# Attention and two expert layers on one core: the second batch's keys and values loaded ahead of the first token group, its first matmuls in halves, the transposes two steps behind the norm

## The chip, the cores and the metric

The program runs as one launch on 1 of the 8 cores of a Trainium2 chip. The metric is the device time of that core in microseconds (us), as the median of three runs. TensorE (PE in the profile, PEld for its weight loads), VectorE (DVE), ScalarE (ACT) and GpSimd (POOL) each take their own instructions in order; SyncE (SP) issues the DMAs.

## The reference, cut to what matters

```python
# attention without softmax, batch 8, 8 heads, 576 tokens, head 64
kv = einsum('bhsd,bhse->bhde', k, v)
out = einsum('bhsd,bhde->bhse', q, kv)
out = out / sqrt(mean(out * out, -1) + 1e-6) * g_norm
x = out.transpose(0, 2, 1, 3).reshape(4608, 512)
# dense layer, 512 -> 2048 -> 512
x = square(maximum(x @ w_in, 0)) @ w_out
# one of 8 experts for each token, 512 -> 1024 -> 512
logits = x @ w_gate + modality_bias[modality_id]
e = argmax(logits); gate = max of softmax(logits)
out = gate * (maximum(x @ w1[e], 0) @ w2[e])
```

All data are float32. The kernel computes a product as three matmuls: each operand is split into a high and a low part (tiles of type fp32r), and high x high, high x low and low x high are summed.

## The kernel before, in words

**Groups and steps.** The 4608 tokens are 36 tiles of 128. `BLK` sorts them into twelve groups j = 0 to 11, of 4, 3, 3, 3, 2 and then 3 tiles each. The dense layer runs group by group. A group has 16 steps i (one for each 128 of the 2048 hidden features). A step issues `emit_h(j, i)` on PE, 12 matmuls whose moving side is the whole group (512 columns in group 0, L368), and `emit_x(j, i - 2)`, 12 matmuls of 512 columns in group 0 (3 for each token tile, L416 to L418), which add feature block i - 2 to the output. Between the two stand, on ACT, `relu` (L385) and `square` (L395, L397), and on DVE `rest` (L403, in the middle groups L402 too), which makes the low part that the third matmul of `emit_x` reads. In group 0 `relu`, `square` and `rest` of feature block i - 1 are issued in step i, between pieces of weight conversion. The results of `emit_h` lie in a PSUM pool of two buffers (`ps_h`), so `emit_h` of block i + 2 waits for `relu` of block i.

**Weights.** w_in and w_out arrive in 32 pieces of 512 KB, alternating, in four buffers `wq`. Numbered n, piece 2i + 1 holds the w_in part that `emit_h(0, i + 1)` reads, piece 2i + 2 the w_out part of `emit_x(0, i)`. Each piece goes through a conversion: `w_scale` (L287 on ACT, for every fourth piece L290 and L291 too), `w_join` (L300, or L304 and L305, on DVE), `w_sum` (L314 on DVE; after it the buffer is free and SP issues the load of piece n + 4), and `w_part`, the high part on ACT (L329) and the low part on DVE (L327). In group 0 step i converts pieces 2i + 4 and 2i + 5 and begins 2i + 6 and 2i + 7.

**Attention.** Before group 0 a prologue loads k and v of batch 0 (four DMAs of 480 KB, L138, and two remainders of 192 KB, L147), multiplies them (`kv_mm`, L153), and makes the four token tiles of group 0 (`att_out` L196, `att_sq` L202, `att_sum` L206, the norm, L239 on DVE for two tiles and L592 on POOL for two, and `att_tr`: four transposes on PE, L252, then L255 on ACT and L256 on DVE, which write the high and low halves of the tile `xt`). `warm` issues matmuls without use. k and v of batch 1 are loaded during steps 0 and 1 of group 0 and multiplied in steps 1 and 2. For every group the tiles of the next are made during its steps: the n-th at step i0 the load of q, at i0 + 2 `att_one` (L196, L202, L206 and two POOL instructions), at i0 + 3 the norm (L239), at i0 + 4 the transposes, with i0 = 3n + 4 in group 0 and 3n + 3 after it. From group 1 on DVE also computes the router's logits (L440), two or three in each of steps 3 to 14.

**Other DMAs on SP's queue.** In step 2 of group 0 `tab_init` (L604) writes a table of 578 KB to DRAM, in runs of 272 bytes. All DMAs named here are issued by SP, in program order.

After the twelve groups the expert layer works through 40 slots of 128 tokens; nothing in it is touched.

Of the kernel before, what the change touches and what calls it, by code (L numbers as in the profile page):

```python
# [40 lines left out]
NKV = 2  # L41
# [4 lines left out]
def body(ctx: ExitStack, tc: tile.TileContext, qT, kvp, kvr, g_norm, w_in, w_out, mod, wg, wgd, mb, w1, w2, out):  # L46
# [80 lines left out]
    def kv_load(b, hp):  # L127

        n = 4 * (b - 1) + hp
        if b == 0 and hp == 0:  # L130
            early.append(xt_p.tile([128, 4, 2, 4, 128], F32, tag="xt0", name="early"))
        if n == 0:
            early.append(xt_p.tile([128, 3, 2, 4, 128], F32, tag="xt1", name="early"))
        if b < NKV:
            t = early[-1][0:120, n % 3 if b else hp]
        else:
            t = t4_p.tile([120, 2, 4, 128], F32, tag="t4", name="kvt")
        nc.sync.dma_start(out=t, in_=kvp[b, hp])  # L138
        kvin[b, hp] = t
        if hp % 2 == 0:  # L140
            if b == 0:
                t = early[0][0:96, hp // 2, :].rearrange("p (a b c) -> p a b c", a=2, b=2)
            elif b < NKV:
                t = g_p.tile([96, 2, 2, 128], F32, tag="ghl", name="rem")
            else:
                t = one.tile([96, 2, 2, 128], F32, tag="rem", name="rem")
            nc.sync.dma_start(out=t, in_=kvr[b, hp // 2])  # L147
            kvrem[b, hp // 2] = t
# [134 lines left out]
    def w_scale(n, c=2):  # L283

        if n < NP:
            low, up, a = w_at(n, c)
            nc.scalar.activation(out=a.bitcast(F32), in_=up.bitcast(F32), func=AF.Copy, scale=2.0**-112)  # L287
            if n % 4 == 0:
                up = up[:, 0]
                nc.scalar.activation(out=up.bitcast(F32), in_=up.bitcast(F32), func=AF.Sign, bias=tiny)  # L290
                nc.scalar.activation(  # L291
                    out=up.bitcast(I32), in_=up.bitcast(F32), func=AF.Copy, scale=2.0**30, bias=-2.0**30
                )

    def w_join(n, c=2):

        for n in range(n, min(n + c, NP)):
            low, up, a = (t[:, 0] for t in w_at(n, 1))
            if n % 4 == 0:
                nc.vector.scalar_tensor_tensor(  # L300
                    out=a, in0=a, scalar=3, in1=up, op0=ALU.logical_shift_left, op1=ALU.bitwise_or
                )
            else:
                nc.vector.tensor_scalar(out=a, in0=a, scalar1=3, scalar2=None, op0=ALU.logical_shift_left)  # L304
                nc.vector.scalar_tensor_tensor(  # L305
                    out=a, in0=up, scalar=0x80000000, in1=a, op0=ALU.bitwise_and, op1=ALU.bitwise_or
                )
# [49 lines left out]
        nc.sync.dma_start(out=wd[e, pc, :, u], in_=uhl.pop(n))  # L357


    gs = {}  # L360

    def emit_h(j, i):
        xt = xts[j]
        ps = ps_h.tile([128, 512], F32, tag="h", name="hps")
        n = 0
        for k in range(4):
            for wi, xi in ((0, 0), (0, 1), (1, 0)):
                nc.tensor.matmul(  # L368
                    ps[:, 0:128 * BLK[j]], wav[:, i, wi, k, :], xt[:, xi, k, :], start=(n == 0), stop=(n == 11)
                )  # L370
                n += 1
        hps[i] = ps
        if j > 0:
            relu(j, i)
            square(j, i)
            rest(j, i)

    hps = {}

    rs = {}  # L380

# [179 lines left out]
    for T in range(n0):  # L561
        att_out(T, *((ps_acc, "acc") if T < 3 else (ps_sm, "sm")))
        sqs.append(att_sq(T))
        if T == 0:
            w_part(0, False, 1)
        if T == 1:
            w_scale(1, 1)
    for T in range(n0):
        att_sum(sqs[T], ss[:, 8 * T:8 * T + 8])
        if T == 0:  # L570
            w_part(0, True, 1)
        if T == 1:
            w_join(1, 1)
            w_sum(1, 1)
    warm(50)
    xc = []
    for T in (2, 3):
# [1 line left out]
        nc.scalar.activation(out=x, in_=xo[T], func=AF.Copy)  # L579
        xc.append(x)  # L580
    ms = att_rms(ss, n0, True)
    w_part(1, False, 1)
    w_scale(2)
    ri = att_inv(*ms)
    for T in range(n0):
        r = ri[:, 8 * T:8 * T + 8]
# [5 lines left out]
            nc.gpsimd.tensor_tensor(out=x, in0=x, in1=r.unsqueeze(2).to_broadcast([128, 8, 64]), op=ALU.mult)  # L592
    for T in range(n0):
        att_tr(T, *((ps_acc, "acc") if T < 2 else (ps_att, "att")))
    w_part(1, True, 1)
    w_join(2)
    w_sum(2)
# [322 lines left out]
    kv_ld, kv_pr = {}, {}  # L920
    for b in range(1, 8):
        for hp in range(4):
            n = 4 * (b - 1) + hp
            if b < NKV:
                i = n // 2
                kv_ld.setdefault((0, i), []).append((b, hp))
                kv_pr.setdefault((0, i + 1), []).append((b, hp))
            else:
                j = BLOCK[b * 576 // 128] - 1
                kv_ld.setdefault((j, 2 * (hp // 2)), []).append((b, hp))  # L930
                kv_pr.setdefault((j, 2 * (hp // 2) + 2), []).append((b, hp))
# [5 lines left out]
    for j in range(NB):  # L937
        nx = [T for T in range(NTILE) if BLOCK[T] == j + 1]
        for i in range(NF):
            if j == 0:  # L940
                if i == NF - 1:
                    wg_sb = p1b.tile([128, E, 512], F32, tag="wg", name="wg_sb")
                    nc.sync.dma_start(out=wg_sb, in_=wg.unsqueeze(0).to_broadcast([128, E, 512]))
                    bias_init()
            emit_h(j, i)
            if j == 0:
                if i == 2:
                    tab_init()
# [18 lines left out]
            for a in kv_ld.get((j, i), []):  # L967
                kv_load(*a)
            for n, T in enumerate(nx):
                i0 = 3 * n + (4 if j == 0 else 3)  # L970
                if i == i0:
                    q_load(T)
                if i == i0 + 2:
                    att_one(T)
                if i == i0 + 3:
                    att_norm(T)
                if i == i0 + 4:
                    att_tr(T)
            if j > 0 and i >= 2:
                emit_x(j, i - 2)  # L980
# [159 lines left out]
```

## Time and profile before

| | |
|---|---|
| three runs | 1451.18, 1452.71, 1454.43 us, median 1452.71 |
| the profiled execution, its own time | 1453.12 us |
| its span in the trace | 1451.4 us |
| mean granted TensorE clock | 0.989 |
| PE busy | 1405.7 us, 97% of the span |
| DVE, ACT, POOL busy | 765.4, 513.8 and 430.5 us (53%, 35%, 30%) |

The span runs from the first instruction to the last; the rest of the execution's time, 1.7 us, lies outside it. "Granted clock" is the share of full speed (1.00 is 2.4 GHz, 0.50 is 1.2 GHz). Times of rows are microseconds from the start of the span. Engines wait on semaphores; a row of the timeline gives the idle time before the instruction in brackets, and what ended it.

### The profile page before, as it was taken

How to read it: one execution, taken by the hardware profiler on the slowest of the kernel's cores; microseconds unless marked ns; L12 is line 12 of the kernel's file. 1: busy time of each engine (PE TensorE's matmuls, PEld its weight loads, DVE VectorE, ACT ScalarE, POOL GpSimd, SP SyncE). 2: the span in 40 equal slices, each digit the busy share in tenths (PEclk: the TensorE clock that was granted, in tenths of full speed). 3: DMA queues.
4: the chain of work that ended last, by engine and by line, in shares of the span. 5: the costliest groups of instructions: out<-in, count | busy, mean ns of one | idle time of the engine just before them, and what ended most of it. 6: DMA issues, size and time to landing. Idle time of an engine off the chain costs nothing. (4 is left out here: it accounts for less than half of the span.)

```text
span 1451.4 us, 24693 instructions
## 1 busy us (share of the span) xinstructions
PE 1405.7 (97%) x7682; PEld 1213.2 (84%) x7682; DVE 765.4 (53%) x1578; ACT 513.8 (35%) x946; POOL 430.5 (30%) x376
## 2 busy tenths in 40 slices
PE   6789999999999999999999999999999999999997
PEld 5578888888998888888888989888888888888886
DVE  4687486858766577766758777162212222212221
ACT  4576234434424344433333443322222222222221
POOL 1003034425415244534334442222222222222210
PEclk9899999999999999999999999999999999999999
DMA  6845235566445565656565651643114623457761
GB/s 182 227 164 182 84 124 189 196 173 218 146 137 196 173 191 188 214 164 197 171 193 189 216 173 68 276 167 140 41 42 155 218 98 103 135 208 254 269 264 75
DMA packets 79440, 246.79 MB, mean 170 GB/s; under 512 B 14670, under 2 KB 14670, under 8 KB 70992
## 3 DMA queue, kind: packets, MB, share of 16 engines
q1 hardware_dynamic: 68176, 208.30, 43.8%
q0 software_dynamic: 8832, 20.09, 4.2%
q10 hardware_dynamic: 2304, 16.78, 2.9%
q8 instruction: 70, 1.15, 0.3%
q14 instruction: 58, 0.48, 0.1%
HBM read 414.33 MB, written 87.70 MB: 346 GB/s over the span
## 5 line engine op out<-in xcount | busy, mean ns | idle before, releaser
L368 PE MATMUL hps<-xt,wa 128*128 128x384 f32 (+2 forms) x2304 | 442.8, 341 | 0.8 <-ACT xt L255 0.8
L368 PEld LDWEIGHTS hps<-xt,wa 128*128 128x128 f32 x2304 | 405.5, 190 | 24.4 <-ACT xt L255 1.2
L352 POOL TENSOR_TENSOR hl<-raw,hl 128x512 fp32r<-128x512 f32 x128 | 177.9, 1396 | 261.6 <-ACT hl L351 261.2
L906 PE MATMUL yps<-wb,hq 128*128 (+1 forms) x960 | 234.2, 399 | 0.4 <-ACT hq L895 0.4
L869 PE MATMUL hps<-wa,xq 128*128 (+1 forms) x960 | 233.7, 399 | 0.0
L416 PE MATMUL acc<-wb,ghl 128*128 128x512 f32 x576 | 231.5, 402 | 0.0
L440 DVE SCALAR_TENSOR_TENSOR junk<-x,wg_sb 128x512 f32<-128x512 f32 x264 | 224.6, 851 | 4.8
L418 PE MATMUL acc<-wb,ghl 128*128 128x512 f32 x576 | 227.0, 394 | 0.0
L417 PE MATMUL acc<-wb,ghl 128*128 128x512 f32 x576 | 226.2, 393 | 0.0
L906 PEld LDWEIGHTS yps<-wb,hq 128*128 128x128 f32 x960 | 177.5, 188 | 41.1 <-ACT hq L895 0.7
L869 PEld LDWEIGHTS hps<-wa,xq 128*128 128x128 f32 x960 | 177.3, 188 | 39.6
L402 DVE TENSOR_TENSOR r<-r 128x384 f32<-128x384 f32 (+1 forms) x160 | 106.0, 663 | 184.3 <-ACT ghl L395 183.9
L385 ACT ACTIVATE r<-hps 128x384 f32<-128x384 f32 (+2 forms) x192 | 93.6, 488 | 305.1 <-PE hps L368 297.6
L403 DVE TENSOR_TENSOR ghl<-r,ghl 128x384 fp32r<-128x384 f32 (+2 forms) x192 | 139.8, 728 | 51.5 <-ACT r L397 33.5
L896 DVE TENSOR_TENSOR hq<-htp,hq 128x512 fp32r<-128x512 f32 x80 | 51.5, 686 | 206.0 <-ACT hq L895 206.0
L913 POOL DMA_INDIRECT out<-y,me x40 | 40.7, 1018 | 351.8 <-ACT y L912 287.9
L351 ACT ACTIVATE hl<-raw 128x512 fp32r<-128x512 f32 x128 | 80.1, 626 | 143.2 <-DMA raw<-w 93.6
L418 PEld LDWEIGHTS acc<-wb,ghl 128*128 128x128 f32 x576 | 108.1, 188 | 23.9
L416 PEld LDWEIGHTS acc<-wb,ghl 128*128 128x128 f32 x576 | 108.4, 188 | 18.4 <-issue 0.5
L417 PEld LDWEIGHTS acc<-wb,ghl 128*128 128x128 f32 x576 | 108.4, 188 | 17.8
L395 ACT ACTIVATE ghl<-r 128x384 fp32r<-128x384 f32 (+2 forms) x192 | 100.9, 526 | 6.1
L885 DVE TENSOR_SCALAR hr<-hps 128x512 f32<-128x512 f32 x36 | 24.9, 692 | 141.1 <-PE hps L869 141.1
(152 smaller groups left out, 1077.9 us busy)
## 6 DMA issues: line engine op xcount, KB each, us to landing
wa<-wd SPq DMA_DIRECT2D x148, 1024.0 KB
wb<-wd SPq DMA_DIRECT2D x144, 1024.0 KB
wd<-hl SPq DMA_DIRECT2D x128, 512.0 KB
raw<-w SPq DMA_DIRECT2D x128, 256.0 KB
kvt<-kvp SPq DMA_DIRECT2D x24, 480.0 KB
x2buf<-x SPq DMA_DIRECT2D x36, 256.0 KB
wq<-w_in SPq DMA_DIRECT2D x16, 512.0 KB
wq<-w_out SPq DMA_DIRECT2D x16, 512.0 KB
```

Source lines behind the costliest of these rows:

```text
L352: nc.gpsimd.tensor_tensor(out=hl[:, 1, :].bitcast(F32R), in0=t, in1=hl[:, 0, :], op=ALU.subtract)
L368: nc.tensor.matmul(ps[:, 0:128 * BLK[j]], wav[:, i, wi, k, :], xt[:, xi, k, :], start=(n == 0), stop=(n == 11))
L385: nc.scalar.activation(out=rs[i], in_=hps.pop(i)[:, 0:c], func=AF.Relu)
L395: nc.scalar.activation(out=g2[0], in_=r, func=AF.Square)
L402: nc.vector.tensor_tensor(out=r, in0=r, in1=r, op=ALU.mult)
L403: nc.vector.tensor_tensor(out=g2[1], in0=r, in1=g2[0].bitcast(F32), op=ALU.subtract)
L416: nc.tensor.matmul(a, g2[0][:, sl], wbv[:, i, 0, :], start=(i == 0), stop=False)
L417: nc.tensor.matmul(a, g2[0][:, sl], wbv[:, i, 1, :], start=False, stop=False)
L418: nc.tensor.matmul(a, g2[1][:, sl], wbv[:, i, 0, :], start=False, stop=(i == NF - 1))
L440: nc.vector.scalar_tensor_tensor(out=junk, in0=x2s[j, t], scalar=1.0, in1=wg_sb[:, e, :], op0=ALU.mult, op1=ALU.mult, accum_out=lgs[j][:, ...
L869: nc.tensor.matmul(hp[f], xq[:, xi, k, :], rhs(wa, s, o + 512 * wi), start=(k == 0 and n == 0), stop=(k == 3 and n == 2),)
L906: nc.tensor.matmul(ps, hq[:, hi, k, :], rhs(wb, s, 1024 * k + 512 * wi), start=(k == 0 and n == 0), stop=(k == 7 and n == 2),)
```

## The change

1. k and v of batch 1: the loads of head pairs 0 to 2 (three of 480 KB, both remainders) are issued in the prologue, behind the load of weight piece 4 and ahead of that of piece 5. The fourth head pair stays in step 1, since it reuses the first one's buffer. The products of pairs 0 to 2 are issued in step 1, that of pair 3 in step 3. The two remainders get the tiles "rem" and "qt" instead of one of the three "ghl" buffers.
2. The prologue's conversion is put in another order: piece 0 takes the DVE path (L304, L305) instead of ACT's L290 and L291; piece 1 is scaled behind the square root, joined behind the first transposed tile and summed behind the matmuls of `emit_h(0, 0)`.
3. `emit_h(0, 0)` is issued in two halves of 256 tokens, ahead of the rest of the conversion.
4. The transposes of every later tile stand at i0 + 5, two steps behind the norm, and i0 is 3n + 3 in group 0 as in the others.

```diff
@@ -140,8 +140,8 @@
         if hp % 2 == 0:
             if b == 0:
                 t = early[0][0:96, hp // 2, :].rearrange("p (a b c) -> p a b c", a=2, b=2)
-            elif b < NKV:
-                t = g_p.tile([96, 2, 2, 128], F32, tag="ghl", name="rem")
+            elif b < NKV and hp > 0:
+                t = one.tile([96, 2, 2, 128], F32, tag="qt", name="rem")
             else:
                 t = one.tile([96, 2, 2, 128], F32, tag="rem", name="rem")
             nc.sync.dma_start(out=t, in_=kvr[b, hp // 2])
@@ -285,7 +285,7 @@
         if n < NP:
             low, up, a = w_at(n, c)
             nc.scalar.activation(out=a.bitcast(F32), in_=up.bitcast(F32), func=AF.Copy, scale=2.0**-112)
-            if n % 4 == 0:
+            if n % 4 == 0 and n > 0:
                 up = up[:, 0]
                 nc.scalar.activation(out=up.bitcast(F32), in_=up.bitcast(F32), func=AF.Sign, bias=tiny)
                 nc.scalar.activation(
@@ -296,7 +296,7 @@
 
         for n in range(n, min(n + c, NP)):
             low, up, a = (t[:, 0] for t in w_at(n, 1))
-            if n % 4 == 0:
+            if n % 4 == 0 and n > 0:
                 nc.vector.scalar_tensor_tensor(
                     out=a, in0=a, scalar=3, in1=up, op0=ALU.logical_shift_left, op1=ALU.bitwise_or
                 )
@@ -357,25 +357,26 @@
         nc.sync.dma_start(out=wd[e, pc, :, u], in_=uhl.pop(n))
 
 
+    hps = {}
     gs = {}
 
-    def emit_h(j, i):
+    def emit_h(j, i, a=0, b=512):
         xt = xts[j]
-        ps = ps_h.tile([128, 512], F32, tag="h", name="hps")
+        b = min(b, 128 * BLK[j])
+        if a == 0:
+            hps[i] = ps_h.tile([128, 512], F32, tag="h", name="hps")
         n = 0
         for k in range(4):
             for wi, xi in ((0, 0), (0, 1), (1, 0)):
                 nc.tensor.matmul(
-                    ps[:, 0:128 * BLK[j]], wav[:, i, wi, k, :], xt[:, xi, k, :], start=(n == 0), stop=(n == 11)
+                    hps[i][:, a:b], wav[:, i, wi, k, :], xt[:, xi, k, a:b], start=(n == 0), stop=(n == 11)
                 )
                 n += 1
-        hps[i] = ps
         if j > 0:
             relu(j, i)
             square(j, i)
             rest(j, i)
 
-    hps = {}
 
     rs = {}
 
@@ -563,15 +564,12 @@
         sqs.append(att_sq(T))
         if T == 0:
             w_part(0, False, 1)
-        if T == 1:
-            w_scale(1, 1)
     for T in range(n0):
         att_sum(sqs[T], ss[:, 8 * T:8 * T + 8])
-        if T == 0:
+        if T == 1:
             w_part(0, True, 1)
-        if T == 1:
-            w_join(1, 1)
-            w_sum(1, 1)
+    for hp in range(3):
+        kv_load(1, hp)
     warm(50)
     xc = []
     for T in (2, 3):
@@ -579,8 +577,7 @@
         nc.scalar.activation(out=x, in_=xo[T], func=AF.Copy)
         xc.append(x)
     ms = att_rms(ss, n0, True)
-    w_part(1, False, 1)
-    w_scale(2)
+    w_scale(1, 1)
     ri = att_inv(*ms)
     for T in range(n0):
         r = ri[:, 8 * T:8 * T + 8]
@@ -592,6 +589,13 @@
             nc.gpsimd.tensor_tensor(out=x, in0=x, in1=r.unsqueeze(2).to_broadcast([128, 8, 64]), op=ALU.mult)
     for T in range(n0):
         att_tr(T, *((ps_acc, "acc") if T < 2 else (ps_att, "att")))
+        if T == 0:
+            w_join(1, 1)
+    emit_h(0, 0, 0, 256)
+    emit_h(0, 0, 256, 512)
+    w_sum(1, 1)
+    w_part(1, False, 1)
+    w_scale(2)
     w_part(1, True, 1)
     w_join(2)
     w_sum(2)
@@ -920,11 +924,10 @@
     kv_ld, kv_pr = {}, {}
     for b in range(1, 8):
         for hp in range(4):
-            n = 4 * (b - 1) + hp
             if b < NKV:
-                i = n // 2
-                kv_ld.setdefault((0, i), []).append((b, hp))
-                kv_pr.setdefault((0, i + 1), []).append((b, hp))
+                if hp == 3:
+                    kv_ld.setdefault((0, 1), []).append((b, hp))
+                kv_pr.setdefault((0, 3 if hp == 3 else 1), []).append((b, hp))
             else:
                 j = BLOCK[b * 576 // 128] - 1
                 kv_ld.setdefault((j, 2 * (hp // 2)), []).append((b, hp))
@@ -942,7 +945,8 @@
                     wg_sb = p1b.tile([128, E, 512], F32, tag="wg", name="wg_sb")
                     nc.sync.dma_start(out=wg_sb, in_=wg.unsqueeze(0).to_broadcast([128, E, 512]))
                     bias_init()
-            emit_h(j, i)
+            if (j, i) != (0, 0):
+                emit_h(j, i)
             if j == 0:
                 if i == 2:
                     tab_init()
@@ -967,14 +971,14 @@
             for a in kv_ld.get((j, i), []):
                 kv_load(*a)
             for n, T in enumerate(nx):
-                i0 = 3 * n + (4 if j == 0 else 3)
+                i0 = 3 * n + 3
                 if i == i0:
                     q_load(T)
                 if i == i0 + 2:
                     att_one(T)
                 if i == i0 + 3:
                     att_norm(T)
-                if i == i0 + 4:
+                if i == i0 + 5:
                     att_tr(T)
             if j > 0 and i >= 2:
                 emit_x(j, i - 2)
```

**The order on SP.** First the rows of the kernel before, from the load of piece 8 to the table:

```order
L272 DMA wq<-w_out 128x1024
L272 DMA wq<-w_in 128x1024
L138 DMA early<-kvp 120x1024
L147 DMA rem<-kvr 96x512
L138 DMA early<-kvp 120x1024
L272 DMA wq<-w_out 128x1024
L272 DMA wq<-w_in 128x1024
L138 DMA early<-kvp 120x1024
L147 DMA rem<-kvr 96x512
L138 DMA early<-kvp 120x1024
L604 DMA tab<-ini 2176x1x68
```

Between pieces 8 and 9 and the table stand four loads of keys and values, two remainders and pieces 10 and 11. Now the rows of the change, from the load of piece 4 to that of piece 5, and from that of piece 8 to the table:

```order
L272 DMA wq<-w_out 128x1024
L138 DMA early<-kvp 120x1024
L147 DMA rem<-kvr 96x512
L138 DMA early<-kvp 120x1024 x2
L147 DMA rem<-kvr 96x512
L272 DMA wq<-w_in 128x1024
```

```order
L272 DMA wq<-w_out 128x1024
L272 DMA wq<-w_in 128x1024
L272 DMA wq<-w_out 128x1024
L272 DMA wq<-w_in 128x1024
L138 DMA early<-kvp 120x1024
L608 DMA tab<-ini 2176x1x68
```

Three of the four loads and both remainders have moved ahead of piece 5; one load is left between piece 11 and the table.

**The order on DVE in group 1**, from the norm of a tile (L239) to its transposed copy (L256); `junk` is the logits' work. First before, then with the change (L402, L403 and L440 are L403, L404 and L441 there):

```order
L239 TENSOR_TENSOR x<-ops,ri 128x512
L440 SCALAR_TENSOR_TENSOR junk,lg<-x_1286,wg_sb 128x512 x2
L402 TENSOR_TENSOR r<-r 128x384
L403 TENSOR_TENSOR ghl<-r,ghl 128x384
L256 SCALAR_TENSOR_TENSOR xt<-tps,gp,xt 128x4x128
```

```order
L239 TENSOR_TENSOR x<-ops,ri 128x512
L441 SCALAR_TENSOR_TENSOR junk,lg<-x_1297,wg_sb 128x512 x2
L403 TENSOR_TENSOR r<-r 128x384
L404 TENSOR_TENSOR ghl<-r,ghl 128x384
L441 SCALAR_TENSOR_TENSOR junk,lg<-x_1297,wg_sb 128x512 x3
L403 TENSOR_TENSOR r<-r 128x384
L404 TENSOR_TENSOR ghl<-r,ghl 128x384
L256 SCALAR_TENSOR_TENSOR xt<-tps,gp,xt 128x4x128
L206 TENSOR_REDUCE ss<-sq 128x8
```

The copy now stands one step further behind the norm, beside the reduction of the next tile. On PE the transposes move by the same step.

## Rows read from the trace of the kernel before

**Rows 1.** The page, busy time, share and instructions of each engine.

```profile
PE 1405.7 (97%) x7682; PEld 1213.2 (84%) x7682; DVE 765.4 (53%) x1578; ACT 513.8 (35%) x946; POOL 430.5 (30%) x376
```

**Rows 2.** Waits, 0 to 106 us, PE: total us, times, longest us.

```profile
PE kvps L153 <- DMA early<-kvp: 17.0, 6, 8.5
```

**Rows 3.** Waits, 105 to 1451 us, PE.

```profile
PE tps L252 <- DVE x L239: 10.8, 18, 1.1
```

**Rows 4.** Timeline of PE: start, us, instruction, count [idle before].

```profile
32.43 8.09 PE L368 MATMUL hps<-xt,wa 128*128 128x512 f32 x24 [0.78 <-ACT xt L255]
...
48.99 1.12 PE L153 MATMUL kvps<-early 120*64 120x64 f32 x16 [8.47 <-DMA early<-kvp]
...
53.19 5.03 PE L368 MATMUL hps<-xt,wa 128*128 128x512 f32 x12
```

**Rows 5.** Timeline of SP's queue, loads of pieces 7 and 10, the table.

```profile
37.77 0.38 SPq L272 DMA_DIRECT2D wq<-w_in  x1
...
48.30 0.35 SPq L272 DMA_DIRECT2D wq<-w_out  x1
...
50.56 0.60 SPq L604 DMA_DIRECT2D tab<-ini  x1
```

**Rows 6.** Timeline of ACT, group 0.

```profile
42.44 1.12 ACT L287 ACTIVATE conv<-wq 128x1024 f32<-128x1024 f32 x1 [3.98 <-DMA wq<-w_in]
...
44.49 0.59 ACT L385 ACTIVATE r<-hps 128x512 f32<-128x512 f32 x1
...
68.30 1.12 ACT L287 ACTIVATE conv<-wq 128x1024 f32<-128x1024 f32 x1 [3.26 <-DMA wq<-w_in]
```

**Rows 7.** Timeline of DVE, `rest` of feature blocks 3, 9 and 12, group 0.

```profile
75.07 0.70 DVE L403 TENSOR_TENSOR ghl<-r,ghl 128x512 fp32r<-128x512 f32 x1
...
113.55 0.71 DVE L403 TENSOR_TENSOR ghl<-r,ghl 128x512 fp32r<-128x512 f32 x1
...
132.07 0.67 DVE L403 TENSOR_TENSOR ghl<-r,ghl 128x512 fp32r<-128x512 f32 x1
```

**Rows 8.** Windows: length, busy times, granted clock, DMA share, GB/s.

```profile
12.00:14.00 2.00, 1.43 (x20) 1.23 (x20) 0.00 (x0) 0.00 (x0) 0.00 (x0) 1.00 1.01 219
60.00:62.00 2.00, 2.00 (x41) 1.57 (x41) 0.58 (x1) 0.00 (x0) 0.00 (x0) 1.00 1.34 116
66.00:68.00 2.00, 2.00 (x10) 1.67 (x9) 0.00 (x0) 0.00 (x0) 0.00 (x0) 1.00 0.93 379
...
102.00:104.00 2.00, 2.00 (x7) 1.52 (x6) 1.93 (x5) 1.97 (x4) 0.00 (x0) 0.50 0.77 256
```

**Rows 9.** Timeline of PE, end of group 0: steps 8, 10, 11, 14, 15.

```profile
100.05 1.12 PE L252 MATMUL tps<-ident,x 128*128 128x128 f32 x4 [3.65 <-DVE x L239]
...
109.32 2.98 PE L368 MATMUL hps<-xt,wa 128*128 128x512 f32 x12
114.85 2.88 PE L368 MATMUL hps<-xt,wa 128*128 128x512 f32 x12
...
132.55 2.88 PE L368 MATMUL hps<-xt,wa 128*128 128x512 f32 x12
...
138.36 3.00 PE L368 MATMUL hps<-xt,wa 128*128 128x512 f32 x12
```

**Rows 10.** Timeline of PE, group 1: its transposes; the start of group 2.

```profile
180.59 0.60 PE L252 MATMUL tps<-ident,x 128*128 128x128 f32 x4
...
194.58 0.63 PE L252 MATMUL tps<-ident,x 128*128 128x128 f32 x4
...
209.14 0.63 PE L252 MATMUL tps<-ident,x 128*128 128x128 f32 x4 [0.48 <-DVE x L239]
...
220.05 2.27 PE L368 MATMUL hps<-xt,wa 128*128 128x384 f32 x12
```

**Rows 11.** Timeline of DVE, the last tile made in group 1.

```profile
208.32 0.68 DVE L239 TENSOR_TENSOR x<-ops,ri 128x512 f32<-128x512 f32 x1
...
211.38 0.74 DVE L256 SCALAR_TENSOR_TENSOR xt<-tps,gp,xt 128x512 fp32r<-128x512 f32 x1
```

## The prediction, on record before the changed kernel ran

> **What bounds the kernel now.** I read the page first: PE is busy for 97% of the span [rows 1], so an edit off PE pays only where PE stands idle. PE's waits then show where that is. In the first 106 us it waits 17.0 us for the loads of batch 1's keys and values, 8.5 us in the longest wait [rows 2]; afterwards 18 times for the norm of a tile about to be transposed, 10.8 us together [rows 3]. The timelines show what stands behind these waits in group 0: `emit_x` of block i cannot start before `rest` of block i, and `emit_h` of block i + 2 not before `relu` of block i has emptied one of two PSUM buffers. `relu` and `rest` stand in order on ACT and DVE between conversions of weight pieces, so a piece that comes late holds PE up. Group 0 thus has two chains: PE's, and the one from DMA through ACT to DVE. From group 1 on only PE's is left, and what ends a wait there ends it for the program.
>
> **Term A, group 0: about 7 us.**
>
> *PE's side.* Before, PE went idle after `emit_h` of blocks 0 and 1 (32.43 + 8.09 = 40.5 us), waited 8.47 us for keys, and began `emit_h(0, 2)` at 53.19 [rows 4]. With three of the four pairs loaded in the prologue that wait goes. What is late next is `relu` of block 0, which ended at 44.49 + 0.59 = 45.1, behind a scaling on ACT that had waited for the DMA of piece 7 [rows 6]; that piece is issued from the same place. So `emit_h(0, 2)` starts at 45.2 at the earliest, 8.0 us sooner.
>
> *The other side.* I walk the DMA queue on to the late piece whose scaling ended its wait at 68.30 [rows 6]. A pair of pieces is 1.05 MB; at the 379 GB/s of the stretch when only pieces move [rows 8] it takes 2.77 us. Piece 7, second of a pair, was issued at 37.77 and scaled at 42.44, so about 1.9 us of it are fixed. A load of keys is 0.49 MB, at the 219 GB/s of the prologue's stretch 2.24 us. The table is 0.59 MB, at 116 GB/s 5.1 us [rows 8]. Piece 10 was issued at 48.30, with 11 and then the table at 50.56 behind it [rows 5]; nothing suggests that it can be issued sooner. Now: 48.30 + 1.9 = 50.2, pair 53.0, the one load left 55.2, the table 60.3, the next pair 63.1. Against 68.30 that is 5.2 us sooner. Piece 5 goes behind the new loads, which I charge with 0.4 us (the 3.98 us wait at 42.44 [rows 6] absorbs the rest), so the chain moves by 4.8.
>
> *The two together.* `rest` of block 3 ended at 75.77 [rows 7] and ends at 71.0. PE could be there at 68, 8.0 earlier than before, or sooner: `emit_h(0, 2)`, 5.03 us long behind the idle time against 2.88 later [rows 4, 9], may lose its slow part. So the conversion decides there. `rest` of block 9 goes from 114.26 to 109.5 [rows 7]. PE began its `emit_x` when `emit_h` of block 11 was through, 114.85 + 2.88 = 117.7 [rows 9]. Moved by 4.8, without the 3.65 us wait of the transposes at 100.05, and without the slow stretch behind it (from there to the next `emit_h` 9.27 us, against 5.53 for a step and 1.12 for the transposes: 2.6 lost [rows 9]), it would be there at 106.6 and waits about 3 us. From 117.7 PE ran without a break to the last `emit_h` at 138.36 [rows 9], 20.7 us: now 130.2. `rest` of block 12 (132.74 before, 127.9 now [rows 7]) stops it for another 0.7, since its `emit_x`, 135.4 before, could start at 127.2. That gives 130.9, 7.4 us sooner, and 0.5 goes back because one attention operation now stands ahead of the conversion on DVE. A is 7. Its bounds: 2.5, if the conversion does not move and only the slow stretch and its wait are cured in part; 8, if the conversion never holds PE up after block 3.
>
> *The prologue's other edits* I cost at nothing. Piece 0 through DVE, the later joins and `emit_h(0, 0)` in halves all bring PE sooner to a point where it waits for `relu` of block 0, held by piece 7 [rows 6]. If that cover were gone they would be worth up to 2.2 us, the two ACT operations that piece 0 no longer needs, at the 1.12 us of a scaling [rows 6]. The halves add 12 matmuls with the same columns in all, beside that wait too.
>
> **Term B, groups 1 to 11: about 12 us.** The 18 waits for the norm take 10.8 us [rows 3]. The norm is issued one step ahead of the transposes, and DVE gets to it late. With two steps it has one step more: transposes in group 1 lay 13.99 us apart (three steps) where none waited, so a step is about 4.7 us, against waits of 1.1 at most [rows 3, 10]. All 18 go. The same three steps took 14.56 where the second transpose waited 0.48 [rows 10], 0.1 more than the wait explains; 18 times that makes 12.6 the upper bound, 10.8 the lower. I take 12, nearer the row with the wait in it.
>
> What the extra step delays is the tile's copy on DVE. For the last tile of group 1 it ended at 211.38 + 0.74 = 212.1 [rows 11]; 4.8 later is 216.9, and group 2 began at 220.05 [rows 10]. 3 us are left, so no new wait.
>
> **The sum.** 7 + 12 = 19. The profiled execution took 1453.12 us, which gives 1434.1; the median of the runs shown stands 0.4 lower, so the forecast is **1433.7**.
>
> **Rivals.**
>
> *The jam stays.* If the fewer loads do not bring the late piece forward (because the table's small writes fill the queue whenever they come: the DMA share there is over 1 at only 116 GB/s [rows 8]), A is its lower bound, 2.5. The sum is 14.5 and the time 1438.2. Against it: two loads and two remainders are gone from between the pieces. Chance 0.11.
>
> *A wait takes the place of the one removed.* If the last tile's copy misses the group's start, each of 11 starts pays about what a norm wait did at its longest, 1.1 us [rows 3]: 12 us, B is nothing, the total 7, the time 1445.7. Against it are the 3 us above. Chance 0.06.
>
> *The whole removed load comes off.* If the queue is served strictly in order and kept full, the late piece comes sooner by all that was taken out ahead of it: three loads at 2.24 and two remainders (0.39 MB together, at 219 GB/s 1.8 us), 8.5 us. PE then sets group 0's end alone: A is 11, the time 1429.7. Against it: piece 10 was issued only at 48.30 [rows 5], when its buffer came free, whatever lay ahead. Chance 0.04. The Trainium skill, "DMA: Bandwidth & Descriptors", section "Queues, rings and completion order", says that each DMA engine consumes the descriptors of a queue in ring order; taken by itself that is this rival, and the row at 48.30 speaks against it.
>
> *PE catches up and loses its clock: slower.* PE now comes earlier than the conversion in steps 3 to 9 and may wait for it there every step. After the 3.65 us wait at 100.05 the granted clock was 0.50 (1.2 GHz) [rows 8, 9], and 2.6 us were lost. If such waits bring it down in each step, the 3 us in hand pay for one; A and B are used up after seven more (7 x 2.6 = 18.2), and from the eighth the kernel is slower, by 2 us or so: 1455. Against it: spread over these steps the waits are about 0.5 us each, and 18 waits of up to 1.1 us later on left the mean clock at 0.989. Chance 0.05: slower 0.03, within the bound 0.02. The Trainium skill, "TensorE: Matmul & The Clock Gate", section "Why this matters for your kernels", warns that idle gaps between bursts of matmuls cost throughput; the trace agrees for the one gap at 100.05, and nothing here shows it for waits of half a microsecond.
>
> That the change doesn't do what it says is possible for the halves alone: on PE they still stand behind all four tiles' transposes. As I count nothing for them, the sum stays.
>
> **How the numbers follow.** The likeliest case has a chance of 0.74. Its own range runs from 1429 (A 8, B 12.6, the prologue's 2.2, and a microsecond of scatter between runs) to 1439.4 (A 2.5, B 10.8). The range 1428.5 to 1441.0 adds the first rival and the third with their scatter and leaves out the second and the slower one. By 0.2%, 2.9 us here, I mean what a measurement of this kernel can tell from no change. Faster is the likeliest case with the first three rivals, 0.95; same 0.02; slower 0.03.
>
> **What would show it.** In the profile after: no wait of PE for keys between 40 and 60 us, and `emit_h(0, 2)` at 45 to 46; ACT's wait for a piece that ended at 68.30 ending at 63 to 64; the last `emit_h` of group 0 at about 131; hardly a row of PE waiting for the norm after 105 us; no wait for `xt` at a group's start. The prediction is wrong in A if the late piece comes as late as before or `emit_h(0, 2)` waits for something else; in B if the waits come back under another name; and altogether if granted clocks of 0.50 show up in steps 3 to 9.

## The result, and the profile after

| | before | changed |
|---|---|---|
| median of four runs | 1452.3 us | 1433.76 us |
| lowest and highest | 1451.18, 1454.43 | 1432.82, 1435.55 |
| profiled execution | 1453.12 | 1432.82 |
| its span | 1451.4 | 1430.8 |
| PE busy | 1405.7 us, 97% | 1399.3 us, 98% |

The ratio is 0.9872 (95% interval 0.9855 to 0.9889): 18.5 us faster, against 19 forecast, and 1433.76 against 1433.7. To see where the time went I read off in both traces when PE begins a group, that is, its first `emit_h`.

| | before | changed | gained |
|---|---|---|---|
| group 1 begins | 143.91 | 136.64 | 7.27 |
| group 11 begins | 866.42 | 846.57 | 19.85 |
| end of the span | 1451.4 | 1430.8 | 20.6 |

So group 0 gained 7.3 us in this pair of executions, groups 1 to 10 together 12.6, and what comes after 0.7, which lies within the scatter of that part (584.2 to 586.9 us in the kernels below). The forecast of the time was met to 0.1 us, which is luck: the runs of the changed kernel alone spread over 2.7 us.

Three views of the changed kernel show the steps (its lines: L371 is `emit_h`, L417 to L419 `emit_x`, L386 `relu`, L404 `rest`). First PE's waits from 105 us on, where the kernel before had 18 for the norm [rows 3]; the columns are us in total, times, longest:

```profile
PE rps L504 <- DVE sb L493: 1.4, 2, 1.2
PE yps L910 <- ACT hq L899: 0.4, 1, 0.4
PE x2ps L451 <- ACT x2t L453: 0.3, 1, 0.3
```

No row of `tps` is left and none names `xt`. The timeline of PE in group 0, and the transposes of group 1 with the start of group 2:

```profile
45.11 5.43 PE L371 MATMUL hps<-xt,wa 128*128 128x512 f32 x12 [7.23 <-ACT r L386]
...
69.66 5.13 PE L371 MATMUL hps<-xt,wa 128*128 128x512 f32 x12 [4.56 <-ACT r L386]
...
131.09 3.00 PE L371 MATMUL hps<-xt,wa 128*128 128x512 f32 x12
136.64 2.27 PE L371 MATMUL hps<-xt,wa 128*128 128x384 f32 x12
...
177.50 0.60 PE L252 MATMUL tps<-ident,x 128*128 128x128 f32 x4
...
191.39 0.60 PE L252 MATMUL tps<-ident,x 128*128 128x128 f32 x4
...
205.26 0.60 PE L252 MATMUL tps<-ident,x 128*128 128x128 f32 x4
```

`emit_h(0, 2)` begins at 45.11, where 53.19 stood in [rows 4], and the wait in front of it is now one for `relu`, not for keys. PE stops once more, 4.56 us ahead of `emit_h(0, 5)`, and then runs on into group 1; the last `emit_h` of group 0 is at 131.09, 138.36 in [rows 9]. The transposes lie 13.89 and 13.87 us apart, with no wait in front of any.

The timeline of ACT, with the scaling of the late piece (68.30 in [rows 6]) and `relu` of block 3 behind it, on which `emit_h(0, 5)` waits; then two rows of DVE, `rest` of blocks 3 and 9 (75.07 and 113.55 in [rows 7]):

```profile
44.48 0.58 ACT L386 ACTIVATE r<-hps 128x512 f32<-128x512 f32 x1
...
64.72 1.12 ACT L287 ACTIVATE conv<-wq 128x1024 f32<-128x1024 f32 x1 [6.74 <-DMA wq<-w_in]
...
69.01 0.60 ACT L386 ACTIVATE r<-hps 128x512 f32<-128x512 f32 x1
```

```profile
71.47 0.67 DVE L404 TENSOR_TENSOR ghl<-r,ghl 128x512 fp32r<-128x512 f32 x1
...
108.40 0.68 DVE L404 TENSOR_TENSOR ghl<-r,ghl 128x512 fp32r<-128x512 f32 x1
```

The late piece comes 3.6 us sooner, `rest` of block 3 too, `rest` of block 9 by 5.2 (rows 113.55 and 108.40).

### The profile page after: what moved, and what is told of

Its sections match the earlier page's. It is cut to its first block, busy times and chain, and to the rows that moved or that the text cites. A ratio compares the mean times of both kernels' runs of the same rounds, so it can differ in the third digit from the quotient of the medians.

```text
span 1430.8 us, 24716 instructions
## 1 busy us (share of the span) xinstructions
PE 1399.3 (98%) x7694; PEld 1213.2 (85%) x7694; DVE 757.1 (53%) x1579; ACT 508.8 (36%) x944; POOL 432.8 (30%) x376
## 5 line engine op out<-in xcount | busy, mean ns | idle before, releaser
L371 PE MATMUL hps<-xt,wa 128*128 128x384 f32 (+2 forms) x2316 | 441.4, 339 | 13.3 <-ACT r L386 11.8
L371 PEld LDWEIGHTS hps<-xt,wa 128*128 128x128 f32 x2316 | 404.9, 190 | 38.0 <-ACT r L386 12.3
L441 DVE SCALAR_TENSOR_TENSOR junk<-x,wg_sb 128x512 f32<-128x512 f32 x264 | 231.2, 876 | 4.8
L417 PE MATMUL acc<-wb,ghl 128*128 128x512 f32 x576 | 229.6, 399 | 0.0
L419 PE MATMUL acc<-wb,ghl 128*128 128x512 f32 x576 | 227.3, 395 | 0.0
L403 DVE TENSOR_TENSOR r<-r 128x384 f32<-128x384 f32 (+1 forms) x160 | 104.4, 653 | 175.8 <-ACT ghl L396 175.6
L386 ACT ACTIVATE r<-hps 128x384 f32<-128x384 f32 (+2 forms) x192 | 93.3, 486 | 237.0 <-PE hps L371 233.7
L404 DVE TENSOR_TENSOR ghl<-r,ghl 128x384 fp32r<-128x384 f32 (+2 forms) x192 | 124.9, 650 | 47.9 <-ACT r L398 30.0
L419 PEld LDWEIGHTS acc<-wb,ghl 128*128 128x128 f32 x576 | 108.1, 188 | 24.1 <-DVE ghl L404 0.6
L417 PEld LDWEIGHTS acc<-wb,ghl 128*128 128x128 f32 x576 | 108.6, 189 | 18.6 <-issue 0.3
L916 ACT ACTIVATE y<-yps,me 128x512 f32<-128x512 f32 x40 | 27.5, 687 | 202.8 <-PE yps L910 192.0
```

The costliest lines, as they stand in the source:

```text
L371: nc.tensor.matmul(hps[i][:, a:b], wav[:, i, wi, k, :], xt[:, xi, k, a:b], start=(n == 0), stop=(n == 11))
L386: nc.scalar.activation(out=rs[i], in_=hps.pop(i)[:, 0:c], func=AF.Relu)
L403: nc.vector.tensor_tensor(out=r, in0=r, in1=r, op=ALU.mult)
L404: nc.vector.tensor_tensor(out=g2[1], in0=r, in1=g2[0].bitcast(F32), op=ALU.subtract)
L417: nc.tensor.matmul(a, g2[0][:, sl], wbv[:, i, 0, :], start=(i == 0), stop=False)
L419: nc.tensor.matmul(a, g2[1][:, sl], wbv[:, i, 0, :], start=False, stop=(i == NF - 1))
```

## The experiments

Twelve runs in three lots; the kernels of a lot shared a chip and its runs of the kernel before, whose medians were 1454.19 (1450.3 to 1459.6), 1453.35 and 1452.8 us. Ratios are to these.

**The transposes alone.**

```diff
-                if i == i0 + 4:
+                if i == i0 + (4 if j == 0 else 5):
                     att_tr(T)
```

> The kernel before, with only the transposes of groups 1 to 10 two steps behind the norm; group 0 is left as it was. Theory: this is term B alone. Group 1 starts at 143.9 us as before, no PE wait for the norm is left behind it, and the time is before less 12.6 to 13.3 us, 1439 to 1440. Rival (part of the gain behind group 0 comes from the loads, or the waits come back at the groups' starts): less than 9 us of gain, 1443 or more.

1439.49 us (1438.9 to 1439.7), ratio 0.9892 (0.9862 to 0.9922). Group 1 begins at 143.96, group 11 at 853.24: 709.3 us for groups 1 to 10, where the kernel before took 722.5. PE's waits from 105 us on:

```profile
PE rps L503 <- DVE sb L492: 1.2, 1, 1.2
PE yps L906 <- ACT hq L895: 0.4, 1, 0.4
PE x2ps L450 <- ACT x2t L452: 0.3, 1, 0.3
```

The theory holds: in the profiles term B is 13.2 us by itself, with group 0 as it was, and it comes neither from the loads nor back at the groups' starts. By the medians of the lot it is 14.7 us, against a kernel before whose runs spread over 9 us.

**The loads alone.** The kernel before with the new `kv_load` calls, `kv_ld`, `kv_pr` and remainder tiles, nothing else; the cut shows the calls.

```diff
+    for hp in range(3):
+        kv_load(1, hp)
     warm(50)
```

> The kernel before with only the loads of the second batch's keys and values moved into the prologue. Theory: emit_h(0, 2) at 45 to 46 us, the late piece scaled at 64.7 to 66.3, the waits for the norm all still there; group 1 starts at 138 to 141 and the time is 3 to 6 us under the kernel before, 1446 to 1450. Rival (the loads alone gain nothing without the other parts): group 1 at 143 or later, 1451 to 1454.

1448.84 us (1448.3 to 1450.9), ratio 0.9965 (0.9951 to 0.9978), so 4.5 us. Group 1 begins at 139.99. PE's timeline in group 0:

```profile
45.62 5.49 PE L368 MATMUL hps<-xt,wa 128*128 128x512 f32 x12 [2.81 <-ACT r L385]
...
70.72 5.26 PE L368 MATMUL hps<-xt,wa 128*128 128x512 f32 x12 [4.67 <-ACT r L385]
...
97.56 0.66 PE L252 MATMUL tps<-ident,x 128*128 128x128 f32 x4 [1.25 <-DVE x L239]
```

The place of both stops is the changed kernel's, with the old prologue. The third row is the one to learn from: the wait of 3.65 us at 100.05 [rows 9] has shrunk to 1.25 with the transposes still one step behind the norm. PE comes to them at 96.3 us, as before (100.05 - 3.65 = 96.4), since the stop for `relu` and its slow matmuls took back what it had gained; the norm is what came sooner, by 2.5 us, with the conversion that it shares DVE with. Its row in the kernel before and then here:

```profile
99.31 0.68 DVE L239 TENSOR_TENSOR x<-ops,ri 128x512 f32<-128x512 f32 x1
```

```profile
96.82 0.68 DVE L239 TENSOR_TENSOR x<-ops,ri 128x512 f32<-128x512 f32 x1
```

**The transposes put back.**

```diff
-                i0 = 3 * n + 3
+                i0 = 3 * n + (4 if j == 0 else 3)
...
-                if i == i0 + 5:
+                if i == i0 + 4:
```

> The changed kernel with the transposes of all groups put back to one step behind the norm (the loads, the prologue and the halves stay). Theory: group 0's gain has two sources. The loads bring emit_h(0, 5) to 69.7 us as in the changed kernel, 3.6 earlier than before; the wait for the norm in step 8 (3.65 us before) and its slow stretch come back, so group 1 starts at about 140.3 and not at 136.6, and the time is 1433.8 + 12.6 + 3.6 = 1450. Rival (group 0's gain is the loads' alone): group 1 starts at 136.6 to 137.2, and the time is 1446 to 1447.

1454.53 us (1450.6 to 1456.6), ratio 1.0 (0.9983 to 1.0016). The profiled execution, the fastest of its ten, took 1450.59 as forecast, but by other parts: group 1 began at 138.1, between theory and rival, and groups 1 to 10 took 725.7 us, 3.2 more than before. The waits for the norm are back and larger: 13.1 us in 17 from 105 us on, the longest 2.6, where the kernel before had 10.8 in 18 and the one with the loads alone 11.7 in 18. Kernels with the transposes one step behind took 722.5 to 725.7 us for groups 1 to 10, those two steps behind, with their tiles where they were, 709.3 to 710.3. Why the median of this kernel lies above that of the loads alone isn't settled; the other waits in its groups were not followed one by one. By its runs the loads, the prologue and the halves were worth nothing on this chip while the transposes stood one step behind, so that the split of the gain into 7 and 12 us rests on the profiles and not on the medians.

**The old prologue.** The changed kernel with piece 0 through ACT's L290 and L291 again, pieces 1 and 2 converted in the old places, and `emit_h(0, 0)` undivided in the loop.

```diff
-    emit_h(0, 0, 0, 256)
-    emit_h(0, 0, 256, 512)
...
-            if (j, i) != (0, 0):
-                emit_h(j, i)
+            emit_h(j, i)
```

> The changed kernel with the prologue's conversion and the undivided first dense group as before; the loads and the transposes stay changed. Theory: these edits are worth nothing, since emit_h(0, 2) waits for relu of block 0 at 45.1 us in any case; group 1 starts at 136.6 within 0.3, the time is 1433.8 within 1. Rival (the earlier prologue carries part of group 0's gain): up to 2.2 us slower, group 1 at 138 to 139, 1435 to 1436.

1437.2 us (1433.7 to 1438.5), ratio 0.987 (0.9837 to 0.9903), group 1 at 139.83: it looked like the rival. I ran it again beside the changed kernel:

> The changed kernel once more, on the chip of the next three kernels, as their measure. Every theory: 1433.8 within 1.5; group 1 starts at 136.6 within 1 if the late piece's scaling (64.72 us before) repeats, and later by what that piece is late if its time scatters.

> The changed kernel with the old prologue once more. Its first profile had emit_h(0, 2) only 0.34 us later than the changed kernel, but the late piece scaled at 66.27 in place of 64.72 and group 1 at 139.83 in place of 136.64. Theory: the first difference is the prologue's, the rest is a piece that landed late in that execution; within 1.5 us of the changed kernel on the same chip, group 1 at 137 to 138. Rival (the old prologue costs group 0 its lead): 3 us slower than the changed kernel on the same chip again, group 1 at 139 to 140.

The changed kernel 1436.35 (1434.2 to 1439.4), ratio 0.9883 (0.9861 to 0.9905); with the old prologue 1435.9 (1434.7 to 1438.8), 0.988 (0.9857 to 0.9903): no difference that these runs can tell. The second profile of the old prologue, PE and then ACT:

```profile
33.12 7.13 PE L371 MATMUL hps<-xt,wa 128*128 128x512 f32 x23 [0.53 <-DVE xt L256]
44.93 4.47 PE L371 MATMUL hps<-xt,wa 128*128 128x512 f32 x12 [2.78 <-ACT r L386]
...
69.85 5.49 PE L371 MATMUL hps<-xt,wa 128*128 128x512 f32 x12 [5.34 <-ACT r L386]
```

```profile
64.91 1.12 ACT L287 ACTIVATE conv<-wq 128x1024 f32<-128x1024 f32 x1 [7.11 <-DMA wq<-w_in]
```

The dense matmuls begin 4 us later (32.1 against 28.06), `emit_h(0, 2)` at the same time: the prologue's edits shorten work in front of a wait, and nothing of them shows in the time. Of the 3 us in the first pair of profiles, 1.6 were the late piece (scaled at 66.27); the rest came behind it. Three profiles of the changed kernel began group 1 at 136.64, 137.70 and 138.26, two of the old prologue at 139.83 and 138.48. All three lie ahead of both, but profiles of one kernel differ by up to 1.6 us, so a microsecond for the prologue is not ruled out.

**The table's write out of group 0.** It goes to step 2 of group 1, from a buffer of its own.

```diff
-    ini = one.tile([128, 17, 4], I32, tag="x", name="ini")
+    ini = one.tile([128, 17, 4], I32, tag="ini", name="ini")
...
-                if i == 2:
-                    tab_init()
...
+            if (j, i) == (1, 2):
+                tab_init()
```

> The changed kernel with the table's write issued in step 2 of group 1 in place of step 2 of group 0. Theory: the write is what holds the late piece back. ACT's scaling that began at 64.72 us begins at about 59.6, PE's wait of 4.56 us ahead of emit_h(0, 5) and the slow stretch behind it are gone, group 1 starts at about 131.5, and the time is about 1428.7. Rival (the pieces behind it are late anyway, since ACT waits for them again at 76.6, 89.1 and 113.8 us): the conversion falls back to its old course by block 9, group 1 starts at 135.6 to 136.6, and the time is 1433 or more.

1441.27 us (1440.2 to 1443.1), ratio 0.9905 (0.9874 to 0.9936): slower than the changed kernel, none of whose twelve runs took more than 1439.4. PE's timeline in group 0, then ACT's:

```profile
65.77 3.04 PE L371 MATMUL hps<-xt,wa 128*128 128x512 f32 x12 [0.20 <-ACT r L386]
...
117.54 4.61 PE L371 MATMUL hps<-xt,wa 128*128 128x512 f32 x12 [2.52 <-ACT r L386]
...
136.07 2.27 PE L371 MATMUL hps<-xt,wa 128*128 128x384 f32 x12
```

```profile
112.31 1.12 ACT L287 ACTIVATE conv<-wq 128x1024 f32<-128x1024 f32 x1 [4.30 <-DMA wq<-w_in]
```

Half of the theory holds: the write is what held the late piece (scaled at 60.77 now), and the stop of 4.56 us is gone. Of the 3.9 us gained at `emit_h(0, 5)`, 0.6 are left at group 1's start. PE has caught up with the conversion, and stops where a later piece is late. And in group 1 the write delays the next keys and values (PE waits 3.0 us for them, and the granted clock is 0.50 from 162.6 to 166.0 us), which lengthens that group from 75.3 to 80.8 us.

**GpSimd for part of the conversion.** The table's write in step 5 of group 1, and the low part of each w_out piece from piece 4 on made on GpSimd; the cut shows the second edit.

```diff
-                nc.vector.tensor_tensor(out=p[1], in0=w, in1=p[0].bitcast(F32), op=ALU.subtract)
+                (nc.gpsimd if m and n > 2 else nc.vector).tensor_tensor(
+                    out=p[1], in0=w, in1=p[0].bitcast(F32), op=ALU.subtract
+                )
```

> The changed kernel with the table's write in step 5 of group 1 and the low part of each w_out piece (from piece 4 on) made on GpSimd in place of DVE. In the last kernel without the table in group 0, PE reached emit_h(0, 5) at 65.8 in place of 69.7, but lost it again from step 12 on, where DVE had no idle time. Theory: DVE's conversion work sets the end of group 0 then; 0.68 us less of it in each step lets PE run without a break, group 1 starts at 130 to 132, the table costs group 1 nothing in its new place, and the time is 1427 to 1429. Rival (late pieces set it, or GpSimd's longer operation holds the conversion): group 1 at 135 or later, 1433 or more.

1439.0 us (1437.9 to 1441.3), ratio 0.9892 (0.9872 to 0.9912). The theory falls: group 1 began at 138.51. `emit_h(0, 5)` came at 66.70, but from the late piece's scaling (61.75) to the one nine steps on (121.67) it took 6.66 us a step, against 6.44 in the last kernel, which has no table in group 0 either (60.77 to 118.72), and 6.17 in the changed kernel (64.72 to 120.22), where the first of these pieces was held by the table. GpSimd's operation takes 1.36 us where DVE's took 0.68, and the same operation of the w_in pieces, still on DVE, 0.81 in place of 0.69 (means from 62 to 122 us, here and in the last kernel). Less work on DVE, bought with a longer operation beside it, did not quicken the conversion.

**What paces group 0, and a better version.** A pair of buffers is released by `w_sum`, its load is issued (at 84.15 and 84.52 us for one pair of the changed kernel), lands and is scaled at once (at 89.09), and `w_sum` releases it again: a loop. Two edits bear on it: the write behind the last piece, its source in a pool behind all others; and the attention work of group 0 collected in a list `late` and issued behind `w_sum` of the following step. The cut leaves out the new pool and the lines that fill the list.

```diff
-    ini = one.tile([128, 17, 4], I32, tag="x", name="ini")
+    ini = ini_p.tile([128, 17, 4], I32, tag="ini", name="ini")
...
-                if i == 2:
+                if i == 12:
                     tab_init()
...
                 w_sum(2 * i + 4)
+                for f, T in late:
+                    f(T)
+                late = []
```

> The changed kernel a third time, as the measure of the next three on their chip: 1434 to 1437, group 1 at 136.6 to 138.5.

> The changed kernel with the table's write behind the last weight piece (step 12 of group 0), its source in a pool allocated behind the others, so that no other tile's address moves. Theory: conversion's own pace (6.2 to 6.4 us a step) sets group 0's end, and PE, which comes to emit_h(0, 5) at 65.7 in place of 69.7, gives most of that back; group 1 starts about 1 us earlier than in the changed kernel on the same chip, groups 1 to 10 take the same 710 us (the two kernels with the table in group 1 took 714 and 718; the first matmul of emit_x took 244.5 ns there against 240.6), and the time is 1 us under it. Rival (the late piece is what group 0 ends by): 4 us or more under it. Second rival (the write in step 12 delays the loads behind it): group 1 longer than 76.5 us, no gain.

> The changed kernel with the attention work of group 0 (products, norm, transposes of the next tiles) issued behind w_sum of the following step, so that on DVE no attention operation stands ahead of the instruction that releases two weight buffers. Theory (conversion and loads form one loop that paces group 0): the loads of some 9 steps are issued 0.6 to 0.7 us earlier, and group 1 starts 2 to 3 us earlier than in the changed kernel on the same chip. Rival (single pieces that land late decide): within 1 us of it.

> Both of the last two edits together. Theory (the loop paces group 0): the gains add, group 1 starts 3 to 4 us earlier than in the changed kernel on the same chip, and the time is 3 to 4 us under it. Rival: no more than the better of the two alone.

| | median (lowest to highest) | ratio (interval) | group 1 begins |
|---|---|---|---|
| changed kernel | 1434.51 (1432.5 to 1437.9) | 0.9879 (0.9854 to 0.9904) | 138.26 |
| write in step 12 | 1432.01 (1431.4 to 1433.6) | 0.9857 (0.9838 to 0.9876) | 135.23 |
| attention behind `w_sum` | 1433.4 (1432.6 to 1434.5) | 0.9869 (0.9849 to 0.9888) | 137.25 |
| both | 1430.12 (1428.5 to 1431.6) | 0.9842 (0.9822 to 0.9862) | 133.16 |

The runs of each edit alone overlap with the changed kernel's. The write gained 2.5 us, between its theory (1) and its rival (4); the second edit 1.1 and not 2 to 3, which is nearer to its rival, so the loop isn't shown by it alone. Together they gain 4.4 us, and none of their four runs overlaps with the changed kernel's. In these four profiles a step takes, from the late piece's scaling to the one seven steps on, 6.10, 6.10, 6.09 and, with both, 5.94 us. PE's timeline of the two together, and of the write alone:

```profile
47.20 5.49 PE L372 MATMUL hps<-xt,wa 128*128 128x512 f32 x12 [7.18 <-ACT r L387]
...
67.46 2.88 PE L372 MATMUL hps<-xt,wa 128*128 128x512 f32 x12
...
115.56 3.01 PE L372 MATMUL hps<-xt,wa 128*128 128x512 f32 x12 [0.35 <-ACT r L387]
```

```profile
116.86 4.45 PE L372 MATMUL hps<-xt,wa 128*128 128x512 f32 x12 [2.33 <-ACT r L387]
```

With both, the stop near 117 us shrinks from 2.33 to 0.35 us, and the slow matmuls behind it go (4.45 against 3.01). The write alone lets PE run into that stop. What cured it is not shown: the pair of pieces behind it was issued from 105.02 us on with the write alone and from 105.06 on with both, so not earlier, but it landed sooner. ACT's scaling of it, the write alone and then both:

```profile
111.62 1.13 ACT L288 ACTIVATE conv<-wq 128x1024 f32<-128x1024 f32 x1 [4.08 <-DMA wq<-w_in]
```

```profile
110.29 1.15 ACT L288 ACTIVATE conv<-wq 128x1024 f32<-128x1024 f32 x1 [2.71 <-DMA wq<-w_in]
```

This version is the fastest of all that ran.

## Why the prediction was right

**Term B, 12 us.** Right, a little small: 12.6 in the changed kernel's profile, 13.2 where only the transposes moved. All 18 waits went (10.8 us [rows 3]), and each cost (12.6 - 10.8) / 18 = 0.10 to (13.2 - 10.8) / 18 = 0.13 us more than the profile counts as waiting; the working had 0.1 from one pair of rows and chose 12 between 10.8 and 12.6. The slack at the groups' starts was enough, though less than the 3 us of the working: the last copy in group 1 ended at 209.38 + 0.74 = 210.1, and group 2 began at 211.96, 1.8 us later.

```profile
209.38 0.74 DVE L256 SCALAR_TENSOR_TENSOR xt<-tps,gp,xt 128x512 fp32r<-128x512 f32 x1
```

**Term A, 7 us.** Right in sum, 7.3 in the first profile and 6.4 as the mean of three (136.64, 137.70, 138.26 against 143.91), but in part by luck, since its steps were off both ways. The transposes alone left group 1's start at 143.96, so the point of departure repeats. The medians give less: 18.5 us for the whole change and 14.7 for the transposes alone, on other chips, leave 3.8, and the loads alone gave 4.5. In the first profile the 7.3 us are made up so: `emit_h(0, 5)` begins 3.6 us sooner (73.23 against 69.66), and from there on PE runs without a wait; the wait of 3.65 us at 100.05 and its slow stretch of 2.6 are gone, and the new stop's slow matmuls cost 2.25. That is 7.6, and 0.3 of it went elsewhere. The working had 4.8 for the first of these and took 3 and 0.7 off for waits that did not come. The row of `emit_h(0, 5)` in the kernel before:

```profile
73.23 2.88 PE L368 MATMUL hps<-xt,wa 128*128 128x512 f32 x12
```

Of its steps:

- `emit_h(0, 2)` at 45.2, set by `relu` of block 0 and not by keys: 45.11. And with the same place of that `relu`, the prologue's edits showed nothing in the runs (1436.35 with them and 1435.9 without, on one chip). The slow part of `emit_h(0, 2)`, which the working thought might go, stayed: 5.43 us, 5.03 before.
- The waits for keys that the working starts from, 17.0 us [rows 2], were misread. Four of the six, 6.9 us, come before 16 us and are for batch 0's keys, which the change leaves where they were; batch 1's are 10.1 us. The sum went by the timeline, so nothing hangs on it. Waits from 30 to 106 us in the kernel before, then from 0 to 106 us in the changed one:

```profile
PE kvps L153 <- DMA early<-kvp: 10.1, 2, 8.5
```

```profile
PE kvps L153 <- DMA early<-kvp: 6.3, 4, 2.4
```

- The conversion sooner by 4.8: mis-sized. The late piece was scaled at 64.72, 3.6 sooner. The table's write was walked near enough: in the trace its 2176 packets of 272 bytes take 7 us and not 5.1, but begin at 53.5 and end at 60.5, where the working had 60.3. What the working sized too small is the pair behind the table, 2.77 us: from the table's last packet to the scaling it took 4.2, and in the kernel before 4.3 (64.0 to 68.30). So the working set a walked time, 63.1, against a measured one. Walked in the same way, with two loads and a remainder in front of the table, the kernel before comes to 66.2 in place of 68.30, and the difference is 3.1. SP's queue shows that the table holds the issue of the pair behind it too: the issue of its first piece took 6.17 us before and 1.98 with the change, and 0.33 in the kernels with no table in front. The first row is the kernel before, the others the changed one:

```profile
53.96 6.17 SPq L272 DMA_DIRECT2D wq<-w_out  x1
```

```profile
54.36 1.98 SPq L272 DMA_DIRECT2D wq<-w_out  x1
56.45 0.37 SPq L272 DMA_DIRECT2D wq<-w_in  x1
```

  Four windows of the changed kernel (length, busy times, clock, DMA share, GB/s): from 56 to 58 us almost all that moves is the table, then the pair comes in beside it:

```profile
56.00:58.00 2.00, 2.00 (x10) 1.65 (x10) 1.97 (x5) 1.92 (x4) 0.00 (x0) 1.00 1.30 146
58.00:60.00 2.00, 2.00 (x27) 1.45 (x26) 2.00 (x3) 0.00 (x0) 0.00 (x0) 1.00 1.28 156
60.00:62.00 2.00, 2.00 (x11) 1.63 (x9) 0.41 (x1) 0.00 (x0) 0.00 (x0) 1.00 1.09 239
62.00:64.00 2.00, 2.00 (x10) 1.69 (x9) 0.00 (x0) 0.00 (x0) 0.00 (x0) 1.00 0.92 354
```

- Where PE waits: wrong in place. I had waits at block 3, at block 9 (3 us) and at block 12 (0.7). There was one of 4.56 us at `emit_h(0, 5)`, for `relu` of block 3 and not for its `rest`, with 2.25 us of slow matmuls behind it (5.13 against 2.88), and after it none (in the third profile one of 1.40, at `emit_h(0, 13)`). `rest` of block 9 ended at 109.08 (109.5 forecast), 1 us before PE came to it (107.18 + 2.88, the `emit_h` in front). Up to that stop the conversion set the course, as argued; behind it PE's own work did.
- The 3.65 us wait in step 8 and its slow stretch, 6.3 us in the working: those I credited in full to PE's side. With the loads alone that wait fell to 1.25. So most of that wait goes with the loads, and the transposes' extra step in group 0 is worth little: group 1 begins at 139.99 with the loads alone, at 138.48 and 139.83 with the loads and all transposes.

**The rivals.** The jam that stays (2.5 for A) did not come, nor did the queue that gives up all 8.5 us: the late piece, at 68.30 by the first, 59.8 by the second and 63 to 64 by the forecast, was scaled at 64.72. The wait that takes the place of the one removed did not come either: no row names `xt` after 105 us, and 1.8 us were left. The one that PE catches up and loses its clock is partly true: with the stop of 4.56 us the granted clock was 0.50 (1.2 GHz) between 70 and 72 us, as with the stop at 100.05 before [rows 8]. That is in step 5, so the sign by which the working would call itself wrong altogether did show up, once.

```profile
70.00:72.00 2.00, 2.00 (x6) 1.54 (x6) 2.00 (x3) 1.97 (x4) 0.00 (x0) 0.50 0.00 0
```

The only other fall in group 0 lies at the wait of 7.23 us ahead of `emit_h(0, 2)`, where the kernel before had one too. The new one cost 2.25 us, and the wait and slow stretch that went from 100.05 paid for it. In two kernels without the table in group 0 a stop of 2.3 to 2.5 us at 117 us brought the granted clock to 0.50 and made the next matmuls 1.6 to 1.7 us longer. Through a stop of 2.42 us in the kernel with GpSimd, a wait of 2.58 with the transposes put back and waits for the norm of up to 1.8 with the loads alone it stayed at 1.00. What decides between these isn't settled. The Trainium skill ("TensorE: Matmul & The Clock Gate", section "Why this matters for your kernels") warns that idle gaps between bursts of matmuls cost throughput. The trace agrees for the stop of 4.56 us, with 5.13 us for matmuls that take 2.88 elsewhere.

## What to carry to other kernels

Split a stage by which chain sets its end, and cost an edit only on that chain: the loads whose longest wait was 8.5 us gave 4.5 when they were moved alone, because the piece that held PE up next came only 2.5 us sooner (65.78 against 68.30), and an earlier prologue gave nothing that the runs could tell. Where one engine waited again and again for another that was merely late in its queue, one more step of lag was worth every wait in full and a little more; the slack at the stage's end has to be read first. When a time walked through a queue is compared, walk the kernel before in the same way and compare the two. A change in a stage that is paced by loads must be measured in several executions; profiles of one kernel differed by up to 1.6 us there.

## What the runs showed that I had not expected

- Two kernels with the table's source as one more tile in the pool `one` ran slower in groups that hold neither the table nor the conversion. The first matmul of `emit_x` took 404 ns there (403 in the kernel with GpSimd) in place of 399, as the groups of the page show for the first of them and for the kernel with the source behind all other pools:

```profile
L417 PE MATMUL acc<-wb,ghl 128*128 128x512 f32 x576 | 232.7, 404 | 0.0
```

```profile
L418 PE MATMUL acc<-wb,ghl 128*128 128x512 f32 x576 | 229.7, 399 | 0.0
```

  The mean alone doesn't tell it, since the kernel before has 402 too. The length of a group does: group 7 took 71.37 us in both kernels, and 71.09 in each of the nine others that have the transposes two steps behind. What differs in the program there is the address of the tiles behind it, 272 bytes on; that this is the cause was argued and not varied further.
- The landing of single weight pieces scatters: in the third profile of the changed kernel the scaling at 115.41 had waited 3.68 us, in the first the one in its place 2.24. What those loads met was not found.
